# Softmax rows kept in SBUF, one undivided dq product, and seven zero stores at other places in the order of SP

## The chip, the cores and the metric

The kernel runs on one core of a Trainium2 chip. The core has five engines with an instruction stream each: TensorE (PE, with its weight loads as PEld), VectorE (DVE), ScalarE (ACT), GpSimd (POOL) and SyncE (SP). SP issues nearly all DMAs of this kernel, in program order; 16 DMA engines carry them out. SBUF is the memory on chip, with 128 partitions; PSUM takes the results of matmuls, and DVE or ACT copies ("evicts") them to SBUF. The metric is the time of one execution on the device in microseconds. Three runs of the kernel before took 430.75, 432.07 and 433.14 us; the median is 432.07. The profile is of one more execution.

## What is computed

Two layers of attention and two of a dense network, all with the same weights, for one token, forward and backward:

```
def _A_ref(x, k_cache, v_cache, wq, wo):        # Hq 32, Hkv 4, Dh 128, W 4096 of Sk 32768
    q = (x @ wq) as heads
    k, v = the last W rows of k_cache and v_cache, each for 8 heads
    p = softmax(q k^T * Dh ** -0.5)
    return (p v) @ wo
def _B_ref(x, w1, b1, w2):                      # D 1024, F 3584
    h = x @ w1 + b1
    return (h * tanh(softplus(h))) @ w2
x = x + _A_ref(layernorm(x), ...)   # A1
x = x + _B_ref(layernorm(x), ...)   # B2
x = x + _A_ref(layernorm(x), ...)   # A3
x = x + _B_ref(layernorm(x), ...)   # B4
outputs: x, and the gradients of x, k_cache, v_cache, wq, wo, w1, b1, w2 for a given grad_out
```

The gradients are large: dwq and dwo have 8.4 MB each, dw1 and dw2 7.3 MB each in bf16. Those of the caches have 33.6 MB each. Only their last 4096 rows of each head are computed (4.2 MB each); the other 58.7 MB are zeros that have to be written.

## The kernel before

**Stages.** The order of all instructions is written out by hand. It runs A1 forward (`attn_fwd`), B2 forward (`mlp_B2_fwd`), A3 forward, B4 forward and backward together (`mlp_B4`), A3 backward (`attn_bwd`), B2 backward (`mlp_B2_bwd`), A1 backward, and then the weight gradients as outer products. In the profile, B2 forward lies at about 70 to 111 us, A3 forward at 112 to 148, B4 at 148 to 219, A3 backward at 219 to 247, B2 backward at 247 to 295, A1 backward from 295 on. Products with one token are memory-bound: each weight matrix is read once for one column. In the stages from A3 on PE also transposes matrices in SBUF (`T8`, `fill`), which the backward products need.

**Zero stores.** The 112 pieces of zeros, 512 KB each, are `zero_jobs`. `zeros(n)` (L140) issues the next n of them on SP, from a place in SBUF that holds zeros (`zsrc`). They have no due time, so they are placed by hand wherever DMA has room: after loads, between blocks of B4 (`ZB4`), between steps of the attention (the `Z_` lists), between chunks of the w2 pass (the dictionary passed to `w2_pass`, L598), and between pieces of the w1 pass (L849).

**Loads.** Weights are loaded in an order that is fixed in `queue`. A load is issued as soon as its slot in a ring of buffers is free (`rel`, `pump`). SP issues in order, so a load stands behind all zero stores that were put before it, and at most eight DMAs of SP are under way, since each waits for the eighth before it.

**w2 pass and w1 pass.** `w2_pass` goes over w2 in 14 chunks of 512 KB: four matmuls, eight transposes with an ACT eviction, a multiply-and-sum on DVE (L596), then eight matmuls for the chunk before, after which its slot is released and `zeros(Z_.get(c, 0))` is called. The w1 pass of B2 backward goes over w1 in 16 pieces of 448 KB in the same way, with no R product.

**Softmax rows.** The backward pass of an attention layer needs its softmax matrix `p` (128 x 1024 bf16, 256 KB). The tile `misc` has three such places: `sB`, `sA` and `zlo`, the last of which holds zeros. A1 writes p to `sA`, which POOL copies to DRAM (`p1_d`, L551). A3 writes p to `sB`. In A3 backward p of A3 goes to DRAM too (`p3_d`, L787) and p of A1 comes back into `sB` (L788); in A1 backward p of A3 comes back into `wo[:, 0, :]` (L759), since the outer products for dV need both.

**Last stage.** In A1 backward `wo_dead` makes the list `jobs` of outer products. A job is four (`w2`, `w1`) or more matmuls with two contracted rows, into PSUM banks that `p_bank` hands out, and as many evictions of 128 x 512 to a staging buffer, shared between DVE (L896) and ACT (L899) by `ev_out`. When a buffer is full, SP stores it (L984 for dw2, L1002 for dw1, L1103 for the caches, L971 for dwo, L1007 for dwq). dw2 has 14 jobs, in seven pairs; a pair ends with two stores of 512 KB. Each pair carries one zero store behind it (the `z` of `add`, L1080, issued in `run_jobs`). `out_step` (L1110) runs jobs inside A1 backward: step 0 issues eight pieces of zeros as five stores, step 3 runs two jobs, step 4 one job after every eighth matmul of dq (L805 to L811), steps 5 and 6 two each. The rest runs after A1 backward.

**dq** is called here the product of dqpair with wq (L805): 64 matmuls, two for each head, that accumulate in the bank `R`. `d_cols` (L404) evicts R and folds it; the backward layer norm follows.

Of the kernel before, what the change touches and what calls it, by code (L numbers as in the profile page):

```python
# [21 lines left out]
def kernel(  # L22
# [42 lines left out]
    keep = ctx.enter_context(tc.tile_pool(name="keep", bufs=1))  # L65
    dram = ctx.enter_context(tc.tile_pool(name="dram", bufs=1, space=bass.MemoryType.DRAM))
    pt = ctx.enter_context(tc.tile_pool(name="pt", bufs=3, space=bass.MemoryType.PSUM))
# [18 lines left out]
    jk = kt([P, WC], BF16, "jk")  # L86
    misc = kt([P, 3072], BF16, "misc")
    sB, sA, zlo, zt = misc[:, 0:1024], misc[:, 1024:2048], misc[:, 2048:3072], misc[:, 1024:3072]
    Kf = K[:].rearrange("p g t d -> p g (t d)")
    Kl = K[:].rearrange("p g t d -> p (g t d)")  # L90
    Vf = V[:].rearrange("p g t d -> p g (t d)")
    kpf = kp[:].rearrange("p j x -> p (j x)")
    jkf = jk[:].bitcast(FP32)

# [5 lines left out]
    v_v = A_v_cache[0, :, Sk - W:, :].rearrange("g (p t) d -> p g t d", p=P)  # L100
    p1_d = dram.tile([P, WC], BF16, name="p1_d")
    p3_d = dram.tile([P, WC], BF16, name="p3_d")

# [19 lines left out]
    make_identity(nc, ident_bf[:])  # L123
    ident_f = kt([P, P], FP32, "ident_f")
    make_identity(nc, ident_f[:])
    nc.gpsimd.memset(zlo, 0.0)
# [176 lines left out]
    gmask = kt([P, G], FP32, "gmask")  # L303
    pat = kt([P, NC, 32], FP32, "pat")
    npair = kt([P, 4, TD], BF16, "npair")
# [16 lines left out]
    def constants():  # L322
        nc.vector.reduce_sum(fold[:], ident_f[:].rearrange("p (c x) -> p x c", c=NC), axis=AX.X)
        nc.vector.tensor_copy(pat[:], fold[:, None, :].to_broadcast([P, NC, 32]))
# [12 lines left out]

    wt = {}
    wk_n = dict(h=TF, hm=TF, u=TF, w_=TF, r=TF, t_f=TF, dact=8)
    cols1 = kt([P, 32], FP32, "cols1")  # L340
# [121 lines left out]
    def attn_fwd(x_col, l, first, p_dst, F_, Z_):  # L462
# [41 lines left out]
        mps = sm_tile(1, P)  # L504
        mm(mps[:], nm[:], ident_f[:], True, True)
        m32 = kpf.bitcast(FP32)[0:1, 0:P]
        nc.vector.tensor_reduce(out=m32[:].rearrange("p (c x) -> p c x", c=NC),
# [11 lines left out]
        tps = sm_tile(P, 1)  # L519
        mm(tps[:], pat[:].rearrange("p c x -> p (c x)"), sw[:], True, True)  # L520
        rT = wk("rT", 1)
# [28 lines left out]
        if first:  # L550
            nc.gpsimd.dma_start(p1_d[:], sA)  # L551
            rel("r2", 0)
# [13 lines left out]

    def mish(h, a_bf, dact, n):
        hm, u, w_, r = wk("hm", n), wk("u", n), wk("w_", n), wk("r", n)
        t_f, v1, v2 = wk("t_f", n), hm, w_
        nc.vector.tensor_scalar(out=hm[:], in0=h, scalar1=20.0, scalar2=None, op0=ALU.min)  # L570
        nc.scalar.activation(u[:], hm[:], ACT.Exp)
        nc.vector.scalar_tensor_tensor(out=w_[:], in0=u[:], scalar=2.0, in1=u[:], op0=ALU.add, op1=ALU.mult)
        nc.vector.tensor_scalar(out=r[:], in0=w_[:], scalar1=2.0, scalar2=None, op0=ALU.add)
        nc.vector.reciprocal(r[:], r[:])
        nc.vector.tensor_mul(t_f[:], w_[:], r[:])
        ga = nc.vector.tensor_mul(a_bf, h, t_f[:])
        nc.vector.scalar_tensor_tensor(out=v1[:], in0=t_f[:], scalar=1.0, in1=r[:], op0=ALU.add, op1=ALU.mult)
# [58 lines left out]
    def mlp_B2_fwd(x_col):  # L636
# [13 lines left out]
        zeros(2)  # L650
        h = wk("h", TF)
        nc.vector.tensor_add(h[:], hacc[:], b1_f[:])
        dact = kt([P, TF], FP32, "dact_B2")
        mish(h[:], apair[:, 1, :], dact[:], TF)
        sv["dact"] = dact
        R, dps, ds = w2_pass(apair[:, 1, :], gpair[:, LI["B4"], :], {8: 1, 9: 1, 10: 1, 11: 1})
        nc.gpsimd.memset(sA, 0.0)
        zsrc[:] = [zt, 2048]
        da4 = kt([P, TF], FP32, "da4")
# [6 lines left out]
    def mlp_B4(x_col, da4):  # L666
# [23 lines left out]
        def sel(b):  # L690
            full = b < 3
            nh, nk = (2, 8) if full else (1, 4)
            hps = sm_tile(P, 8)
            for cc in range(2):
                for tt in range(2):
                    k = 2 * cc + tt
                    mm(hps[:, k:k + 4 * (nh - 1) + 1:4], jkf[:, cc * 256 + tt:cc * 256 + tt + 255:2], selD[:] if full else sel1[:], k == 0, k == 3)
            h = wk("h", nk)
            nc.vector.tensor_add(h[:], hps[:, 0:nk], b1_f[:, 8 * b:8 * b + nk])
            hcol[b] = h  # L700

        def act(b):
            nk, f0 = 8 if b < 3 else 4, 8 * b
            dact = wk("dact", nk)
            mish(hcol[b][:], apair[:, 0, f0:f0 + nk], dact[:], nk)
            nc.vector.tensor_mul(hpair[:, 0, f0:f0 + nk], da4[:, f0:f0 + nk], dact[:])
            nc.vector.tensor_mul(dh[:, f0:f0 + nk], da4[:, f0:f0 + nk], dact[:])
            spent(2.8, 0.2)
# [34 lines left out]
        for i in range(2):  # L743
            mm(dn[:].rearrange("p (a i) -> p i a", i=2)[:, i, :], jkf[:, i * P:(i + 1) * P], ident_f[:, 0:P:32], i == 0, i == 1)
        tt = wk("xx", 2 * TD)
# [3 lines left out]
    def attn_bwd(g_col, g_bf, l, sv, last, nxt, F_, Z_, step):  # L749
# [6 lines left out]
        if last:  # L756
            p_t, ds_t = sB, wo[:, 1, :]
            wo_dead()
            nc.gpsimd.dma_start(wo[:, 0, :], p3_d[:])  # L759
        else:  # L760
            p_t, ds_t = sv["p"], sA
        zeros(Z_[0])
        acc = one_tile("acc", HQ)
        j_cols(big, acc, 8, F_[0], True)
        do32 = wk("do32", HQ)
        nc.vector.tensor_copy(pad[:, :, 0:8], acc[:].rearrange("p (g h) -> p g h", g=G))
# [18 lines left out]
        sv["p"], sv["ds"] = p_t, ds_t  # L785
        if not last:
            nc.gpsimd.dma_start(p3_d[:], sB)  # L787
            nc.gpsimd.dma_start(sB, p1_d[:])  # L788
            sv["p"] = wo[:, 0, :]
        step(1)  # L790
# [14 lines left out]
        for h in range(HQ):  # L805
            for hf in range(2):
                g = 2 * hf + h % 2
                mm(R[32 * g:32 * g + 32, :].rearrange("p (t d) -> p t d", t=4), bc(dqpair[:, LI[l], h:h + 1]),
                   wq[:, 4 * hf:4 * hf + 4, h * P:(h + 1) * P], h < 2, h >= HQ - 2, tile_position=(0, 32 * g))
            if h % 4 == 3 and h < 31:  # L810
                step(4)  # L811
        y = d_cols(R, hook=lambda: step(5))
# [4 lines left out]
    def mlp_B2_bwd(g_col, g_bf, sv, x3):  # L817
        bcast_g(g_bf)
        R, dps, ds = w2_pass(apair[:, 0, :], g_bf, {10: 1})
        zeros(3)  # L820
        dh = kt([P, TF], FP32, "dh_B2")
# [21 lines left out]
        def pairs(i, w, ring, sl):  # L843
# [4 lines left out]
            rel(ring, sl)  # L848
            zeros({9: 2, 12: 1, 14: 1}.get(i, 0))  # L849

# [9 lines left out]
        n3 = nv[:].rearrange("p (t h) -> p t h", h=2)  # L860
        t3 = wk("t3", TD)
        nc.vector.tensor_add(t3[:], n3[:, :, 0], n3[:, :, 1])
# [171 lines left out]
    def wo_dead():  # L1034
# [43 lines left out]
        for n in range(NW2 // 2):  # L1078
            add("w2a", n, lambda c=2 * n: pair_half(row_sp["w2"], c, w2_out, w2_lhs, 0))
            add("w2", n, lambda c=2 * n: pair_half(row_sp["w2"], c, w2_out, w2_lhs, 1), 1)  # L1080
        for n in range(16):
# [28 lines left out]
    def out_step(i):  # L1110
# [62 lines left out]
```

## Time and profile before

| | us |
|---|---|
| median of 3 runs | 432.07 |
| profiled execution | 431.02 |
| its span, first to last instruction | 429.2 |
| busy: PE, DVE, ACT | 321.2, 234.4, 219.1 |
| q1, SP's DMA queue, 168.84 MB: share of the 16 engines' span | 99.2% |
| one dw2, dwo or dk/dv store (512 KB), median to landing | 9.4 (all from wo), 7.1 (K) |
| chain: share of DMA, PE, ACT, DVE | 40%, 35%, 11%, 7% |
| last eviction ends | 413 |

A DMA's time to landing has its time in the queue in it. The DMA share in the windows is the time that packets took, as a share of 16 engines; it does not tell slow packets from full ones, so it is read together with the GB/s. The releaser of a wait is inferred from semaphores.

### The profile page before, as it was taken

The numbers are of one execution on the slowest core, as the hardware profiler recorded it, in microseconds if no ns is written. First come the engines' busy times: TensorE is split into PE (matmuls) and PEld (weight loads), VectorE is DVE, ScalarE is ACT, GpSimd is POOL, SyncE is SP. The second block draws the span as 40 slices with busy tenths as digits, with TensorE's granted clock in tenths as the row PEclk, the third lists the DMA queues.
The fourth block names the chain that finished last, engine by engine and source line by source line (L and its number), as shares of the span: only waits on it lengthen the run. The fifth ranks groups of instructions, "written<-read, shape, count | busy, mean of one in ns | idle before, by whom it ended". The sixth has DMA issues, their size and how long they took to land.

```text
span 429.2 us, 9216 instructions
## 1 busy us (share of the span) xinstructions
PE 321.2 (75%) x3732; PEld 188.3 (44%) x3732; DVE 234.4 (55%) x532; ACT 219.1 (51%) x335; POOL 15.4 (4%) x54
## 2 busy tenths in 40 slices
PE   3476736367697898878788898887799799999830
PEld 1154315345455587756646565764423223321100
DVE  2035102068535346555537288673367998899940
ACT  1036101036436356646534267482487699999940
POOL 2000000000000000000000000000400111000000
PEclk9999555569889979999989989685955555555555
DMA  8999999999999999999999999999999999999995
GB/s 329 423 419 419 411 408 399 406 407 378 387 418 409 417 417 365 417 409 384 381 408 406 350 397 386 373 362 421 411 421 417 419 413 413 403 409 412 410 413 242
DMA packets 49975, 170.50 MB, mean 397 GB/s; under 512 B 4848, under 2 KB 5900, under 8 KB 45836
## 3 DMA queue, kind: packets, MB, share of 16 engines
q1 hardware_dynamic: 49456, 168.84, 99.2%
q0 software_dynamic: 416, 1.06, 0.7%
q8 instruction: 29, 0.48, 0.4%
q14 instruction: 14, 0.11, 0.1%
q10 hardware_dynamic: 60, 0.01, 0.0%
HBM read 70.79 MB, written 99.10 MB: 396 GB/s over the span
## 4 chain that ended last, share of the span: by engine, by line
DMA 40%; PE 35%; ACT 11%; DVE 7%; issue 3%; SPq 0%; ACTq 0%; DVEq 0%
DMA K<-in_B_w_dram 9%; DMA wo<-in_A_wo_dram 8%; PE tp L264 8%; PE R L244 7%; DMA out_dram<-misc 7%; DMA K<-in_A_k_cache_dram 5%; DMA wo<-in_B_w_dram 4%; PE sm L244 4%; PE acc L244 4%; ACT wo L899 4%; PE op L244 3%; ACT K L237 3%; PE lo L244 3%; DMA out_dram<-wo 3%; ACT wq L899 3%
## 5 line engine op out<-in xcount | busy, mean ns | idle before, releaser
L237 ACT COPY K<-tp 128x1024 bf16<-128x1024 bf16 x60 | 58.8, 1016 | 14.3 <-PE tp L264 13.3
L264 PE MATMUL tp<-ident_bf,K 128*128 128x128 bf16 x656 | 52.0, 238 | 6.4 <-ACT K L237 2.8
L244 PE MATMUL op<-wo 2*128 2x512 bf16 (+2 forms) x123 | 52.1, 562 | 5.0 <-ACT wo L899 2.7
L244 PEld LDWEIGHTS <-wo 128*128 128x128 bf16 (+2 forms) x590 | 24.4, 101 | 61.8 <-issue 53.5
L264 PEld LDWEIGHTS <-K 128*128 128x128 bf16 x656 | 44.3, 109 | 12.7 <-issue 9.6
L237 ACT COPY wo<-tp 128x1024 bf16<-128x1024 bf16 x33 | 33.5, 1023 | 25.7 <-PE tp L264 22.9
L899 ACT CAST wo<-op 128x512 bf16<-128x512 f32 (+1 forms) x51 | 31.2, 629 | 7.9 <-DMA out_dram<-wo 1.8
L596 DVE CUSTOM_DVE_ANT_0 K<-K,kp 128x1024 bf16<-128x1024 bf16 (+1 forms) x22 | 24.6, 1127 | 2.8 <-PE R L244 1.0
L235 DVE COPY jk<-R 128x512 f32<-128x512 f32 (+1 forms) x11 | 7.3, 665 | 33.9 <-PE R L244 33.9
L264 PE MATMUL tp<-ident_bf,wo 128*128 128x128 bf16 x336 | 24.4, 226 | 0.6 <-ACT wo L237 0.5
L244 PE MATMUL acc<-wo 2*128 2x512 bf16 (+1 forms) x41 | 24.3, 593 | 0.2 <-DVE V L896 0.2
L244 PE MATMUL hi<-wo 2*128 2x512 bf16 x41 | 24.3, 592 | 0.0
L244 PE MATMUL lo<-wo 2*128 2x512 bf16 x41 | 24.1, 587 | 0.0
L264 PEld LDWEIGHTS <-wo 128*128 128x128 bf16 x336 | 20.1, 101 | 6.9 <-issue 6.8
L237 ACT CAST jk<-hi 128x512 bf16<-128x512 f32 x4 | 2.6, 661 | 37.7 <-PE hi L244 37.7
L244 PE MATMUL sm<-wo 2*128 2x512 bf16 (+1 forms) x33 | 19.8, 600 | 1.3 <-DVE cols L384 1.3
L896 DVE CAST wo<-op 128x512 bf16<-128x512 f32 (+1 forms) x32 | 18.4, 599 | 4.1 <-PE tp L930 1.5
L235 DVE CAST jk<-lo 128x512 bf16<-128x512 f32 x4 | 2.8, 711 | 31.9 <-PE lo L244 31.9
L235 DVE COPY K<-tp 128x1024 bf16<-128x1024 bf16 x22 | 14.9, 690 | 9.6 <-PE tp L264 9.5
L244 PE MATMUL R<-wo 2*128 2x512 bf16 (+1 forms) x33 | 19.6, 593 | 0.6 <-DVE wo L896 0.4
L237 ACT COPY wq<-tp 128x1024 bf16<-128x1024 bf16 x13 | 13.0, 1018 | 11.7 <-PE tp L264 8.8
L364 ACT ACTIVATE cols<-cols,eps_t 128x1 f32<-128x1 f32 x4 | 1.2, 294 | 33.4 <-DVE cols L361 33.4
(293 smaller groups left out, 656.2 us busy)
## 6 DMA issues: line engine op xcount, KB each, us to landing
out_dram<-misc SPq DMA_DIRECT2D x97, 512.0 KB, 10.2
out_dram<-wo SPq DMA_DIRECT2D x39, 512.0 KB, 9.4
K<-in_B_w_dram SPq DMA_DIRECT2D x28, 512.0 KB, 8.1
K<-in_A_k_cache_dram SPq DMA_DIRECT2D x9, 1024.0 KB, 14.9
wq<-in_A_wq_dram SPq DMA_DIRECT2D x8, 1024.0 KB, 10.0
out_dram<-wq SPq DMA_DIRECT2D x8, 1024.0 KB, 13.5
K<-in_B_w_dram SPq DMA_DIRECT2D x16, 448.0 KB, 6.1
out_dram<-wo SPq DMA_DIRECT2D x16, 448.0 KB, 7.2
```

Source lines behind the costliest of these rows:

```text
L235: return nc.vector.tensor_copy(out_ap, in_ap)
L237: return nc.scalar.copy(out_ap, in_ap)
L244: return nc.tensor.matmul(out_ap, lhsT=lhsT, rhs=rhs, start=start, stop=stop, skip_group_check=True, **kw)
L264: nc.tensor.transpose(ps[:, b * P:(b + 1) * P], ap, ident_bf[:])
L364: nc.scalar.activation(lnv[:], var[:], ACT.Ln, bias=eps_t[:, 0:1], scale=1.0)
L596: return nc.vector.tensor_tensor_reduce(out=w, in0=w, in1=vec, scale=1.0, scalar=0.0, op0=ALU.mult, op1=ALU.add, accum_out=acc_col)
L896: nc.vector.tensor_copy(out_ap, in_ap)
L899: nc.scalar.copy(out_ap, in_ap)
```

## The change

The rows: `misc` gets a fourth place, `sC`, for p of A1; p of A3 stays in `sB`. The tiles in DRAM and the four copies by POOL are gone. To make room, the float identity lies in a part of `kp` and is made again after the B2 forward w2 pass (`make_identity`, on POOL), a 128 x 4 selector `sel4` stands in for its strided use, `pat` is replaced by four products with `fold`, and the temporaries of `mish` and `do32` lie in `kp` and `jk`.

The order: step 4 of `out_step` is no longer called, so the 64 matmuls of dq follow each other, behind the two jobs of step 3. The seven dw2 pairs carry no zero store. One more piece of zeros is issued at chunk 2 of the B2 forward w2 pass, two more in A3 backward after dqpair is set off (Z_[2], 3 to 5), one at chunk 1 of the B2 backward w2 pass, two more between w2 pass and w1 pass (3 to 5), and one at piece 4 of the w1 pass. `ZB4` goes from 12, 11, 9, 7 to 11, 11, 10, 7.

```diff
-    misc = kt([P, 3072], BF16, "misc")
-    sB, sA, zlo, zt = misc[:, 0:1024], misc[:, 1024:2048], misc[:, 2048:3072], misc[:, 1024:3072]
+    misc = kt([P, 4096], BF16, "misc")
+    sB, sA, zlo, zt, sC = misc[:, 0:1024], misc[:, 1024:2048], misc[:, 2048:3072], misc[:, 1024:3072], misc[:, 3072:4096]
-    p1_d = dram.tile([P, WC], BF16, name="p1_d")
-    p3_d = dram.tile([P, WC], BF16, name="p3_d")
-    ident_f = kt([P, P], FP32, "ident_f")
-    make_identity(nc, ident_f[:])
+    ident_f = kpf[:, 512:768].bitcast(FP32)
+    make_identity(nc, ident_f)
+    sel4 = kt([P, 4], FP32, "sel4")
...
-        mm(tps[:], pat[:].rearrange("p c x -> p (c x)"), sw[:], True, True)
+        for c in range(NC):
+            mm(tps[32 * c:32 * c + 32, :], fold[:], sw[:], True, True, tile_position=(0, 32 * c))
...
         if first:
-            nc.gpsimd.dma_start(p1_d[:], sA)
             rel("r2", 0)
...
-    def mish(h, a_bf, dact, n):
-        hm, u, w_, r = wk("hm", n), wk("u", n), wk("w_", n), wk("r", n)
-        t_f, v1, v2 = wk("t_f", n), hm, w_
+    def mish(h, a_bf, dact, n, tmp):
+        hm, u, w_, r, t_f = [tmp[:, i * n:(i + 1) * n] for i in range(1, 6)]
+        v1, v2 = hm, w_
...
-        R, dps, ds = w2_pass(apair[:, 1, :], gpair[:, LI["B4"], :], {8: 1, 9: 1, 10: 1, 11: 1})
+        R, dps, ds = w2_pass(apair[:, 1, :], gpair[:, LI["B4"], :], {2: 1, 8: 1, 9: 1, 10: 1, 11: 1})
         nc.gpsimd.memset(sA, 0.0)
+        make_identity(nc, ident_f)
...
-            p_t, ds_t = sB, wo[:, 1, :]
+            p_t, ds_t = sC, wo[:, 1, :]
             wo_dead()
-            nc.gpsimd.dma_start(wo[:, 0, :], p3_d[:])
...
-        do32 = wk("do32", HQ)
+        do32 = jkf[:, P:P + HQ]
...
-        if not last:
-            nc.gpsimd.dma_start(p3_d[:], sB)
-            nc.gpsimd.dma_start(sB, p1_d[:])
-            sv["p"] = wo[:, 0, :]
...
-            if h % 4 == 3 and h < 31:
-                step(4)
...
-        R, dps, ds = w2_pass(apair[:, 0, :], g_bf, {10: 1})
-        zeros(3)
+        R, dps, ds = w2_pass(apair[:, 0, :], g_bf, {1: 1, 10: 1})
+        zeros(5)
...
-            zeros({9: 2, 12: 1, 14: 1}.get(i, 0))
+            zeros({4: 1, 9: 2, 12: 1, 14: 1}.get(i, 0))
...
-            add("w2", n, lambda c=2 * n: pair_half(row_sp["w2"], c, w2_out, w2_lhs, 1), 1)
+            add("w2", n, lambda c=2 * n: pair_half(row_sp["w2"], c, w2_out, w2_lhs, 1))
...
-            run_jobs(1 if i == 4 else 2)
-
-    ZB4 = [12, 11, 9, 7]
+            run_jobs(2)
+
+    ZB4 = [11, 11, 10, 7]
...
-    x1, sA1 = attn_fwd(x0, "A1", True, sA, [0] * 6, [0] * 4)
+    x1, sA1 = attn_fwd(x0, "A1", True, sC, [0] * 6, [0] * 4)
...
-    g2, g2b, _ = attn_bwd(g3, g3b, "A3", sA3, False, "B2", [4, 3, 5, 2], [3, 1, 3], lambda i: None)
+    g2, g2b, _ = attn_bwd(g3, g3b, "A3", sA3, False, "B2", [4, 3, 5, 2], [3, 1, 5], lambda i: None)
```

More of the change, by code (lines that the diff above doesn't have):

```diff
@@ L65 @@
     keep = ctx.enter_context(tc.tile_pool(name="keep", bufs=1))
-    dram = ctx.enter_context(tc.tile_pool(name="dram", bufs=1, space=bass.MemoryType.DRAM))
     pt = ctx.enter_context(tc.tile_pool(name="pt", bufs=3, space=bass.MemoryType.PSUM))
@@ L92 @@
     kpf = kp[:].rearrange("p j x -> p (j x)")
-    jkf = jk[:].bitcast(FP32)
+    jkf, kpf32 = jk[:].bitcast(FP32), kpf.bitcast(FP32)
     wq_v = A_wq.rearrange("(t p) j -> p t j", p=P)
@@ L303 @@
     gmask = kt([P, G], FP32, "gmask")
-    pat = kt([P, NC, 32], FP32, "pat")
     npair = kt([P, 4, TD], BF16, "npair")
@@ L322, in constants @@
     def constants():
-        nc.vector.reduce_sum(fold[:], ident_f[:].rearrange("p (c x) -> p x c", c=NC), axis=AX.X)
-        nc.vector.tensor_copy(pat[:], fold[:, None, :].to_broadcast([P, NC, 32]))
+        nc.vector.reduce_sum(fold[:], ident_f.rearrange("p (c x) -> p x c", c=NC), axis=AX.X)
+        nc.vector.tensor_copy(sel4[:], ident_f[:, 0:P:32])
         nc.vector.reduce_sum(gmask[:], fold[:].rearrange("p (g h) -> p g h", g=G), axis=AX.X)
@@ L338 @@
     wt = {}
-    wk_n = dict(h=TF, hm=TF, u=TF, w_=TF, r=TF, t_f=TF, dact=8)
+    wk_n = {}
     cols1 = kt([P, 32], FP32, "cols1")
@@ L504, in attn_fwd @@
         mps = sm_tile(1, P)
-        mm(mps[:], nm[:], ident_f[:], True, True)
-        m32 = kpf.bitcast(FP32)[0:1, 0:P]
+        mm(mps[:], nm[:], ident_f, True, True)
+        m32 = kpf32[0:1, 0:P]
         nc.vector.tensor_reduce(out=m32[:].rearrange("p (c x) -> p c x", c=NC),
@@ L650, in mlp_B2_fwd @@
         zeros(2)
-        h = wk("h", TF)
-        nc.vector.tensor_add(h[:], hacc[:], b1_f[:])
+        h = jkf[:, 0:TF]
+        nc.vector.tensor_add(h, hacc[:], b1_f[:])
         dact = kt([P, TF], FP32, "dact_B2")
-        mish(h[:], apair[:, 1, :], dact[:], TF)
+        mish(h, apair[:, 1, :], dact[:], TF, jkf)
         sv["dact"] = dact
-        R, dps, ds = w2_pass(apair[:, 1, :], gpair[:, LI["B4"], :], {8: 1, 9: 1, 10: 1, 11: 1})
+        R, dps, ds = w2_pass(apair[:, 1, :], gpair[:, LI["B4"], :], {2: 1, 8: 1, 9: 1, 10: 1, 11: 1})
         nc.gpsimd.memset(sA, 0.0)
+        make_identity(nc, ident_f)
         zsrc[:] = [zt, 2048]
@@ L697, in sel @@
                     mm(hps[:, k:k + 4 * (nh - 1) + 1:4], jkf[:, cc * 256 + tt:cc * 256 + tt + 255:2], selD[:] if full else sel1[:], k == 0, k == 3)
-            h = wk("h", nk)
-            nc.vector.tensor_add(h[:], hps[:, 0:nk], b1_f[:, 8 * b:8 * b + nk])
+            h = kpf32[:, 64 * (b % 2):64 * (b % 2) + nk]
+            nc.vector.tensor_add(h, hps[:, 0:nk], b1_f[:, 8 * b:8 * b + nk])
             hcol[b] = h
@@ L703, in act @@
             nk, f0 = 8 if b < 3 else 4, 8 * b
[L704 to L707, printed above, removed]
+            tmp = kpf32[:, 64 * (b % 2):64 * (b % 2) + 64]
+            dact = tmp[:, 6 * nk:7 * nk]
+            mish(hcol[b], apair[:, 0, f0:f0 + nk], dact, nk, tmp)
+            nc.vector.tensor_mul(hpair[:, 0, f0:f0 + nk], da4[:, f0:f0 + nk], dact)
+            nc.vector.tensor_mul(dh[:, f0:f0 + nk], da4[:, f0:f0 + nk], dact)
             spent(2.8, 0.2)
@@ L743, in mlp_B4 @@
         for i in range(2):
-            mm(dn[:].rearrange("p (a i) -> p i a", i=2)[:, i, :], jkf[:, i * P:(i + 1) * P], ident_f[:, 0:P:32], i == 0, i == 1)
+            mm(dn[:].rearrange("p (a i) -> p i a", i=2)[:, i, :], jkf[:, i * P:(i + 1) * P], sel4[:], i == 0, i == 1)
         tt = wk("xx", 2 * TD)
@@ L860, in mlp_B2_bwd @@
         n3 = nv[:].rearrange("p (t h) -> p t h", h=2)
-        t3 = wk("t3", TD)
+        t3 = wk("t2", TD)
         nc.vector.tensor_add(t3[:], n3[:, :, 0], n3[:, :, 1])
```

## The prediction

> **What bounds the kernel now.** I read the page first: DMA by slices, the queues, the chain by engine.
>
> ```profile
> GB/s 329 423 419 419 411 408 399 406 407 378 387 418 409 417 417 365 417 409 384 381 408 406 350 397 386 373 362 421 411 421 417 419 413 413 403 409 412 410 413 242
> q1 hardware_dynamic: 49456, 168.84, 99.2%
> q0 software_dynamic: 416, 1.06, 0.7%
> HBM read 70.79 MB, written 99.10 MB: 396 GB/s over the span
> DMA 40%; PE 35%; ACT 11%; DVE 7%; issue 3%; SPq 0%; ACTq 0%; DVEq 0%
> ```
>
> The 16 DMA engines are occupied from the first load to the last store, and most slices move 405 to 423 GB/s: bytes set the time. But six slices lie at 350 to 381, so there is room for stores in some places, and only 40% of the chain is DMA, so other work paces stretches of it. q0 is the queue of the four softmax-row copies. Next, the windows by stage (columns: length, busy us of PE, PEld, DVE, ACT, POOL, then TensorE clock, DMA share, GB/s):
>
> ```profile
> 90.00:115.00 25.00, 18.88 (x290) 13.40 (x290) 20.46 (x47) 14.17 (x14) 0.95 (x1) 0.91 1.01 386
> 235.00:250.00 15.00, 11.92 (x167) 7.52 (x164) 5.75 (x14) 3.39 (x5) 0.55 (x1) 0.93 0.98 365
> 250.00:268.00 18.00, 15.79 (x262) 10.99 (x263) 16.38 (x29) 14.17 (x14) 0.00 (x0) 0.96 1.01 390
> 268.00:292.00 24.00, 19.95 (x268) 17.38 (x268) 16.94 (x37) 15.74 (x17) 0.00 (x0) 0.72 1.01 373
> 303.00:338.00 35.00, 30.54 (x258) 11.33 (x247) 22.67 (x48) 23.22 (x42) 3.10 (x18) 0.64 1.03 418
> 338.00:380.00 42.00, 38.81 (x232) 11.81 (x229) 38.48 (x77) 36.62 (x74) 4.27 (x17) 0.50 1.02 411
> 380.00:413.00 33.00, 28.94 (x115) 5.92 (x112) 31.61 (x52) 33.00 (x68) 0.00 (x0) 0.50 1.02 413
> 413.00:424.50 11.50, 0.00 (x0) 0.00 (x0) 0.00 (x0) 0.06 (x1) 0.00 (x0) 0.50 0.99 405
> ```
>
> The first four rows are the stages that read w2 and w1 for B2, and the dq stage of A3: their rates are 365 to 390. From 303 on the rate is full, and after the engines stop at 413 DMA needs another 11.5 us. But DVE and ACT are nearly full too from 338. Two limits lie close together there. Last, the timeline around dq and the stores:
>
> ```profile
> 240.18 3.64 PE L244 MATMUL R<-wq,dqpair 128*32 128x512 bf16 x64
> 313.79 1.04 PE L244 MATMUL R<-wq,dqpair 128*32 128x512 bf16 x8
> 314.77 0.60 PE L244 MATMUL op<-wo 2*128 2x512 bf16 x1
> 329.42 0.69 DVE L896 CAST wo<-op 128x512 bf16<-128x512 f32 x1 [1.18 <-DMA out_dram<-wo]
> 331.82 1.57 SPq L984 DMA_DIRECT2D out_dram<-wo  x2
> 333.44 1.19 SPq L151 DMA_DIRECT2D out_dram<-wo  x1
> 356.51 4.85 SPq L1103 DMA_DIRECT2D out_dram<-V  x4
> 361.48 4.88 SPq L1002 DMA_DIRECT2D out_dram<-wo  x4
> ```
>
> dq of A3 took 3.64 us in one piece at full clock; dq of A1 runs as eight groups of 8, some 0.97 us apart from the next work, at half clock. Each pair of dW2 chunks is stored with one zero store behind it. Four stores occupy SP for 4.85 us, 1.2 each: SP is held to the pace of the DMA engines (512 KB in 1.25 us). And a DVE eviction waited 1.18 us for a staging buffer that a store still held.
>
> **The change, part by part.** All times on the profiled execution (span 429.2, 431.02 in all, 1.05 under the median 432.07).
>
> *Softmax rows.* Four copies of 256 KB go (L551, L787, L788, L759): 1.05 MB, at 413 GB/s 2.5 us of DMA. Three, 1.9 us, lie before 303; the fourth, 0.6, is at 303. The first lies in 5 to 90 us, which runs at 413 GB/s, so 0.6 us comes straight off. The rest counts as DMA time in the sum.
>
> *Seven zero stores* leave the last stage: 7 x 1.25 = 8.75 us of DMA there. With the row copy the last stage loses 9.35 us of DMA.
>
> *The same seven earlier.* By the order of SP: one between the w2 loads of the B2 forward (about 98 us); the twelve after B4's first block become eleven and the nine after its third ten, so that one store moves some 30 us later and past the loads of block 1 and 2; two more behind the first seven w2 loads of the B2 backward (246 us); one after its chunk 1; two more before the w1 pass (269); one after its piece 4. Loads are queued behind them on SP, and the chain waits for these loads: it has 6.93 us on one of them from 256.4 and 6.94 on one from 282.9. So each store costs 1.25 us unless DMA had room. Room against 415 GB/s: 25 x 29/415 = 1.75 us in the first window, 1.8, 1.1 and 2.4 in the next three, 7.0 in all. How much of that can be filled the trace does not say: slow packets or idle engines look alike in it (share 0.98 to 1.01). Bounds 0 and 7.0. I take 4.35: the one store at 98 fits wholly in its 1.75; half of 2.9 for the three of the w2 pass, whose loads from chunk 7 on already come 1.28 us apart; 1.6 of 2.4 in the w1 pass, where the evictions and not the loads set the pace until 280. So at 303 the chain is late by 8.75 - 1.9 - 4.35 = 2.5 us (bounds 6.85 and -0.15).
>
> *dq in one piece.* Before, the last pair of dW2 is issued at 336.98. After: two jobs on PE (310.9 to 312.4), then 64 matmuls. Between 3.64 us (row of A3) and 8 x 0.97 = 7.8 (half clock). I take 5.4: the clock has just fallen there, and the dense run that starts at 295.77 goes from 0.43 us for each four to 0.22 at 299.14, 3.4 us later; 3.4 us at 0.121 are 28 matmuls, the other 36 take 2.0. The upper bound has a row for it: from 310 to 338 PE was busy 25 of 28 us and the clock stood at 0.55. [...] Dq ends at 317.8, its eight evictions done under it. Then 12 jobs, 48 evictions: DVE starts one each 0.60, ACT each 0.49, so 0.27 together at best; 42 us for 120 in the next stage are 0.35 with all else. At 0.31 they take 14.9; one more for the eviction of R: 333.7. The engines are 3.3 us earlier (bounds -0.5 and 5), and waits for staging buffers such as the 1.18 go with it; I take 3.5. What dq had covered: PE's K=2 products; they are now behind it, and who would wait is DMA. The eight stores of zeros issued at 303.6 hold it until about 320; the next pair of data comes at 321 or so, so up to 1.5 us of DMA may stand idle there.
>
> *What the last stage can give.* From 338 to 380 stores land 7.1 us after issue, some 5.7 in flight at 1.25 each. A cushion of three is needed (at 200 to 205 us, with three left, the rate fell to 321), so 7.1 - 3 x 1.25 = 3.4 us of lag can go before DMA waits for the engines. Dwo and dwq are 16.8 MB, 41 us of DMA, and the engines make them in 33: that phase stays DMA's, and its end moves with its start. So the end moves by 3.5 + 3.4 = 6.9, under the 9.35 that bytes alone would give (bounds 3.4 and 9.35). [...]
>
> *Small edits.* Four 32-column products replace the one with pat (0.25 us of PE each piece, twice in the kernel): +0.3 us each on the softmax sum, beside zero stores in A3 and row loads of wo in A1; without that cover 0.6. Mish's temporaries in kp and jk, sel4 for the strided identity: same counts and shapes, 0. The new identity on POOL (0.5 us) has some 20 us before its reader. The eviction of R now waits for POOL's copy of do too, which in the last stage ends at 304 against 309: 0.
>
> Sum: -6.9 + 2.5 = -4.4 us: 426.6 on the profiled execution, **427.7** against the median.
>
> **Rivals.**
> *Even exchange.* The low rates are slow packets, not room: late by 6.85 at 303, and 6.9 back at the end: 0, 432.0. For it: DMA share near 1.0 in all four windows, and w2 loads already 1.28 us apart. Against: the rate of 331 to 360 from 235 to 245, where SP issued nothing for 6 us.
> *Slower.* The last stage is the engines' own: dq in one piece leaves DVE and ACT idle for 5 us and nothing comes of the staging waits, so the start of dwo does not move, and only the 3.4 us of lag go, while the stores cost their 6.85 earlier: +3.4, 435.5. It decides if dW2's last pair is issued no earlier after dq's start than before (26 us) and less than 3.4 us of room is filled. For it: ACT 33.00 of 33 us. Against: both evicting engines idle 12 of 35 us from 303 to 338, and DVE waits for stores there.
> *Bytes alone.* All 7.0 filled and DMA never waits: -9.4, 422.7. For it: full rate throughout 303 to 413. Against: the cushion.
> *It doesn't do what it says:* the rows could still be held up by a wait for the zero stores that read the same tile. The waits are unchanged but for those of POOL's queue, so I give it 0.02, time as before.
>
> **How the numbers follow.** A measurement of this kernel tells 0.5%, 2.2 us, from no change. Forecast 0.56 (its own range 425 to 430), even exchange 0.17, slower 0.15, bytes alone 0.10, not done 0.02. Faster is 0.56 + 0.10 = 0.66; same 0.19; slower 0.15. The range of 422.5 to 433 holds the first, second and fourth and cuts the outer part of the slower one.
>
> **What would show it.** Queue q0 shrinks from 1.06 MB to the small outputs. In the windows, the B2 backward (w2 and w1) ends 2 to 3 us later relative to its start and moves more GB/s; if it is over 5 us later, the room was not there. Dq is one row of 64 matmuls of 4 to 6 us. The last dW2 store is issued 20 to 24 us after dq's first matmul. After 338 SP's stores wait for evictions and land in under 7.1 us; a tail after the last eviction of 8 to 9 us in place of 11.5. The forecast is wrong if the tail is as long as before, or the start of dwo is no earlier.

## The result, and the profile after

| | before | after |
|---|---|---|
| median, 20 runs each (us) | 432.52 (430.75 to 434.19) | 435.01 (432.45 to 437.97) |
| profiled execution / its span | 431.02 / 429.2 | 436.97 / 435.2 |
| first store of step 0 in A1 backward | 303.6 | 313.9 |
| from there to the last eviction | 109.5 | 107.0 |
| from the last eviction to the end of the span | 16.1 | 14.3 |

The changed kernel is slower: ratio 1.005, 95% interval 1.0033 to 1.0068. The forecast of 427.7 was wrong.

The profiled execution of the changed kernel lies 1.96 us above its median, that of before 1.5 below. So the two traces differ by 6.0 us and the medians by 2.5. Sizes are therefore taken below from experiments whose profiled executions lie within half a microsecond of their medians, where there are such.

The page of the changed kernel: DMA by slices, the queue of the row copies, and the chain by engine (which this time accounts for about half of the span only, so its shares can't be set beside those of before):

```profile
GB/s 318 425 420 416 409 407 397 409 399 364 358 418 404 417 416 384 392 356 388 373 416 404 363 396 391 334 400 419 411 424 358 368 301 404 385 374 410 411 412 323
...
q0 software_dynamic: 96, 0.01, 0.0%
HBM read 70.27 MB, written 98.58 MB: 388 GB/s over the span
...
PE 20%; DMA 13%; ACT 10%; DVE 4%; issue 2%; SPq 1%; ACTq 0%; DVEq 0%
```

The row copies are gone (q0 moved 1.06 MB before). But the rate over the span fell from 396 to 388, the early slices are no fuller, and there are new dips at 358, 368 and 301 from 326 us on, where before every slice but the last moved over 400.

Windows of the changed kernel (columns as before: length, busy us of PE, PEld, DVE, ACT, POOL, clock, DMA share, GB/s). The first four rows are the same stretches as before; the next four are those of before set 10.3 us later, as A1 backward now starts that much later:

```profile
90.00:115.00 25.00, 20.10 (x273) 14.27 (x274) 19.81 (x41) 14.31 (x15) 1.27 (x3) 0.71 0.99 364
235.00:250.00 15.00, 11.87 (x179) 8.03 (x175) 6.48 (x14) 4.74 (x6) 0.00 (x0) 1.00 1.00 375
250.00:268.00 18.00, 13.03 (x184) 8.85 (x184) 12.02 (x22) 9.70 (x10) 0.00 (x0) 0.82 1.03 402
268.00:292.00 24.00, 17.85 (x248) 14.54 (x244) 15.60 (x33) 13.04 (x15) 0.00 (x0) 0.78 0.99 363
313.30:348.30 35.00, 28.93 (x262) 11.58 (x254) 23.86 (x51) 24.20 (x46) 2.51 (x17) 0.73 0.95 385
348.30:390.30 42.00, 39.62 (x232) 12.28 (x231) 38.55 (x77) 37.43 (x77) 4.48 (x17) 0.50 0.93 365
390.30:423.30 33.00, 26.46 (x106) 5.38 (x103) 29.45 (x49) 30.60 (x63) 0.00 (x0) 0.50 1.02 411
423.30:433.00 9.70, 0.00 (x0) 0.00 (x0) 0.00 (x0) 0.00 (x0) 0.00 (x0) 0.50 0.98 401
```

Two things are to be seen. In the w2 pass (250 to 268) the engines got through less: PE 184 matmuls where there were 262, ACT 10 instructions where there were 14. The stores went in, and the loads and the work behind them came later. (Of the delay 2.8 us lie ahead of this stage: its first w2 load is issued at 240.73, before at 237.90.) And in the last stage the DMA engines now wait: 385 and 365 GB/s where it was 418 and 411. The DMA share says the same: it fell from 1.03 and 1.02 to 0.95 and 0.93, which is 35 x 0.08 + 42 x 0.09 = 6.6 us of DMA time that nothing uses, out of the 9.35 us of transfers that were taken away there.

How the stores hold the loads up, in the timeline of SP in the changed kernel (start, length, instructions):

```profile
242.20 3.65 SPq L180 DMA_DIRECT2D K<-in_B_w_dram  x5
246.17 5.58 SPq L147 DMA_DIRECT2D out_dram<-misc  x5
254.38 1.62 SPq L180 DMA_DIRECT2D K<-in_B_w_dram  x2
256.05 0.89 SPq L147 DMA_DIRECT2D out_dram<-misc  x1
257.10 15.97 SPq L180 DMA_DIRECT2D K<-in_B_w_dram  x9
```

The five stores at 246.17 (three before the change) and the one at 256.05 (new) stand ahead of the loads of the next chunks. On DVE, in the same kernel, the multiply-and-sum of the w2 pass shows what follows (the bracket is the idle time before):

```profile
259.48 1.23 DVE L593 CUSTOM_DVE_ANT_0 K<-K,kp 128x1024 bf16<-128x1024 bf16 x1
...
264.19 1.22 DVE L593 CUSTOM_DVE_ANT_0 K<-K,kp 128x1024 bf16<-128x1024 bf16 x1 [3.47 <-PE R L242]
```

DVE stands still for 3.47 us. It waits for PE, and PE for a load, as PE's waits from 245 to 280 say (us in all, times, longest):

```profile
PE R L242 <- DMA K<-in_B_w_dram: 4.5, 3, 3.5
```

The same view of a kernel with the rows kept on chip and the stores where they were (e1_rows_only below):

```profile
PE R L242 <- DMA K<-in_B_w_dram: 0.5, 1, 0.5
```

### The profile page after: what moved, and what is told of

It reads as the page before. It is cut to its first block, busy times and chain, and to the rows that moved or that the text cites. A ratio compares the mean times of both kernels' runs of the same rounds, so it can differ in the third digit from the quotient of the medians.

```text
span 435.2 us, 9224 instructions
## 1 busy us (share of the span) xinstructions
PE 321.5 (74%) x3744; PEld 190.7 (44%) x3744; DVE 233.3 (54%) x532; ACT 218.5 (50%) x335; POOL 13.6 (3%) x52
## 4 chain that ended last, share of the span: by engine, by line
PE 20%; DMA 13%; ACT 10%; DVE 4%; issue 2%; SPq 1%; ACTq 0%; DVEq 0%
DMA out_dram<-misc 7%; ACT wo L891 5%; DMA K<-in_B_w_dram 5%; PE R L242 5%; PE op L242 3%; PE tp L262 3%; ACT wq L891 3%; PE acc L242 3%; DMA K<-in_A_k_cache_dram 2%; PE sm L242 2%; PE lo L242 1%; ACT K L235 1%; PE hi L242 1%; PE tp L922 1%; DVE wo L888 1%
## 5 line engine op out<-in xcount | busy, mean ns | idle before, releaser
L262 PE MATMUL tp<-ident_bf,K 128*128 128x128 bf16 x656 | 53.6, 241 | 9.6 <-DMA K<-in_B_w_dram 4.2
L242 PE MATMUL op<-wo 2*128 2x512 bf16 (+2 forms) x112 | 47.3, 542 | 5.9 <-ACT wo L891 2.5
L242 PEld LDWEIGHTS <-wo 128*128 128x128 bf16 (+2 forms) x558 | 23.0, 102 | 51.3 <-issue 42.9
L262 PE MATMUL tp<-ident_bf,wo 128*128 128x128 bf16 x336 | 26.6, 238 | 0.6 <-ACT wo L235 0.5
L262 PEld LDWEIGHTS <-wo 128*128 128x128 bf16 x336 | 22.1, 107 | 7.6 <-issue 7.3
L242 PE MATMUL hi<-wo 2*128 2x512 bf16 x40 | 23.0, 574 | 0.0
L233 DVE COPY wo<-tp 128x1024 bf16<-128x1024 bf16 x19 | 12.8, 689 | 11.8 <-PE tp L262 11.7
L235 ACT COPY wq<-tp 128x1024 bf16<-128x1024 bf16 x13 | 13.0, 1019 | 11.8 <-PE tp L262 9.0
L242 PE MATMUL R<-wo,operm 128*32 128x512 bf16 x128 | 13.3, 564 | 7.1 <-DMA wo<-in_A_wo_dram 6.8
L242 PE MATMUL acc<-wo 2*128 2x512 bf16 (+1 forms) x32 | 18.3, 572 | 0.0
L242 PEld LDWEIGHTS <-npair 128*32 128x32 bf16 x184 | 5.8, 108 | 26.2 <-issue 21.8
```

What stands on the lines that cost most here:

```text
L233: return nc.vector.tensor_copy(out_ap, in_ap)
L235: return nc.scalar.copy(out_ap, in_ap)
L242: return nc.tensor.matmul(out_ap, lhsT=lhsT, rhs=rhs, start=start, stop=stop, skip_group_check=True, **kw)
L262: nc.tensor.transpose(ps[:, b * P:(b + 1) * P], ap, ident_bf[:])
```

## The experiments

They take the change apart into its three pieces (rows, dq, stores) and then vary the number of stores that are moved. Ratios are to the kernel before, run beside them on the same chip (medians 432.76 for the first four, 432.62 for the others; e1 to e4, e5 to e8 and e9 to e11 ran on three different chips, so between these groups the ratios are the fairer comparison). All points in time in the table are us of the profiled execution: the first store of A1 backward ("late stage starts"), from there to the last eviction, and from there to the end of the span. The column "B2 backward" is the time from the issue of its first w2 load to the start of the late stage. Six of the seven stores are issued inside it, and it leaves out what B4 does.

| kernel | median | ratio (95%) | B2 backward | late stage starts | to last eviction | to the end |
|---|---|---|---|---|---|---|
| before | 432.52 | | 65.7 | 303.6 | 109.5 | 125.6 |
| after | 435.01 | 1.005 (1.0033 to 1.0068) | 73.1 | 313.9 | 107.0 | 121.3 |
| e1: rows alone | 429.75 | 0.9935 (0.9915 to 0.9955) | 65.1 | 302.3 | 109.2 | 125.4 |
| e2: rows and dq | 430.4 | 0.9943 (0.9921 to 0.9965) | 65.1 | 303.2 | 109.5 | 125.5 |
| e3: rows and stores | 435.6 | 1.0074 (1.005 to 1.0098) | 72.6 | 310.3 | 108.7 | 123.1 |
| e4: stores alone | 437.69 | 1.012 (1.0099 to 1.014) | 75.0 | 313.5 | 109.0 | 123.5 |
| e5: rows, three stores, two behind w2 loads | 431.39 | 0.9959 (0.994 to 0.9978) | 68.7 | 308.4 | 108.2 | 122.5 |
| e6: rows, three stores in the w1 pass | 429.9 | 0.9933 (0.9911 to 0.9955) | 71.0 | 307.8 | 107.6 | 121.9 |
| e7: rows, one store in B2 forward | 430.34 | 0.9952 (0.993 to 0.9974) | 65.3 | 303.5 | 108.4 | 124.7 |
| e8: rows, six stores the other way | 436.81 | 1.0086 (1.0053 to 1.0119) | 66.8 | 303.4 | 115.7 | 131.7 |
| e9: after, without the stores of step 0 | 435.29 | 1.0052 (1.003 to 1.0073) | | (about 311) | | |
| e10: after, without the seven stores | 425.28 | 0.9848 (0.9785 to 0.9912) | 65.9 | 302.1 | 107.0 | 121.2 |
| e11: e6 with dq in one piece | 430.64 | 0.9947 (0.9925 to 0.9969) | 68.7 | 304.7 | 107.8 | 122.8 |

e9's start is that of its dq (320.2) less the 8.8 us that lie between the two in the others.

### The three pieces

**e1_rows_only.** The changed kernel with dq in turns again and the seven stores back at the dw2 pairs:

```diff
+            if h % 4 == 3 and h < 31:
+                step(4)
-            add("w2", n, lambda c=2 * n: pair_half(row_sp["w2"], c, w2_out, w2_lhs, 1))
+            add("w2", n, lambda c=2 * n: pair_half(row_sp["w2"], c, w2_out, w2_lhs, 1), 1)
-            run_jobs(2)
+            run_jobs(1 if i == 4 else 2)
-    ZB4 = [11, 11, 10, 7]
+    ZB4 = [12, 11, 9, 7]
...
-        zeros(5)
+        zeros(3)
...
```

Expected:

> The changed kernel with dq interleaved with the dw2 jobs again and all seven zero stores back behind the dw2 pairs, ZB4 12, 11, 9, 7: only the softmax rows stay on chip. Theory A (the stores put earlier cost their DMA time and more there, the row copies were worth their 2.5 us): 2 to 3 us faster than before, ratio 0.993 to 0.995. Theory B (dq in one piece is the loss, by starving DMA in the last stage): the same here, since neither is left. If the row copies were hidden: ratio 1.000.

429.75: 3.0 us faster than before. The rows do what the bytes said, and the new small instructions cost nothing that shows.

**e2_rows_dq.** The stores back at the pairs, dq left in one piece (e1 without the first and third hunk shown). Expected:

> The changed kernel with only the seven zero stores back behind the dw2 pairs (ZB4 as before); dq stays in one piece. Theory A: within 1 us of the kernel with the rows alone, so ratio 0.993 to 0.998. Theory B: slower than the rows alone by 3 us or more, ratio above 1.000.

430.4, no different from e1 within the intervals. With the stores in the pairs, dq in one piece changes nothing: the late stage takes 125.5 us against 125.4.

**e3_rows_zeros.** The changed kernel with dq in turns again (of e1 only the first and third hunk shown). Expected:

> The changed kernel with only dq interleaved again (one dw2 job after every eighth matmul); the seven zero stores stay early. Theory A: still slower than before, ratio 1.003 to 1.008. Theory B: faster than before by 2 us or more, ratio under 0.996.

435.6: from e1 to e3 the seven stores cost 5.85 us in the medians and 5.7 in the traces. The late stage starts 8.0 later, and 2.3 come back in it. Their own DMA time is 8.75. The B2 backward, which holds six of them (7.5 us of DMA), takes 7.5 us more. Its first load and the first store of the late stage, in e1 and then in e3:

```profile
237.21 4.46 SPq L180 DMA_DIRECT2D K<-in_B_w_dram  x7
302.30 3.62 SPq L149 DMA_DIRECT2D out_dram<-wo  x5
...
237.71 6.09 SPq L180 DMA_DIRECT2D K<-in_B_w_dram  x7
310.30 2.64 SPq L149 DMA_DIRECT2D out_dram<-wo  x4
```

**e4_zeros_only.** The kernel before with only the seven stores moved:

```diff
-            add("w2", n, lambda c=2 * n: pair_half(row_sp["w2"], c, w2_out, w2_lhs, 1), 1)
+            add("w2", n, lambda c=2 * n: pair_half(row_sp["w2"], c, w2_out, w2_lhs, 1))
-    ZB4 = [12, 11, 9, 7]
+    ZB4 = [11, 11, 10, 7]
...
-        zeros(3)
+        zeros(5)
...
```

> The kernel before with only the seven zero stores and ZB4 placed as in the changed kernel; rows through DRAM, dq interleaved. Theory A: slower by 3 to 7 us (late by 7 to 10 us at the start of A1 backward, of which 3 to 5 come back at the end), ratio 1.007 to 1.016. Theory B: ratio 0.998 to 1.002, since what leaves the last stage pays for what enters earlier.

437.69, the slowest of all, 4.9 above before. The late stage starts 9.9 us later and gives back 2.1. So the stores alone make the loss, with or without the rows and with or without dq in one piece.

### How many stores, and where

**e5_three_w2, e6_three_w1, e7_one_fwd.** From e1, three, three and one of the seven moves, each with as many pairs that lose their store:

e5:

```diff
-        R, dps, ds = w2_pass(apair[:, 0, :], g_bf, {10: 1})
+        R, dps, ds = w2_pass(apair[:, 0, :], g_bf, {1: 1, 10: 1})
-    g2, g2b, _ = attn_bwd(g3, g3b, "A3", sA3, False, "B2", [4, 3, 5, 2], [3, 1, 3], lambda i: None)
+    g2, g2b, _ = attn_bwd(g3, g3b, "A3", sA3, False, "B2", [4, 3, 5, 2], [3, 1, 5], lambda i: None)
```

e6:

```diff
-        zeros(3)
+        zeros(5)
-            zeros({9: 2, 12: 1, 14: 1}.get(i, 0))
+            zeros({4: 1, 9: 2, 12: 1, 14: 1}.get(i, 0))
```

e7:

```diff
-        R, dps, ds = w2_pass(apair[:, 1, :], gpair[:, LI["B4"], :], {8: 1, 9: 1, 10: 1, 11: 1})
+        R, dps, ds = w2_pass(apair[:, 1, :], gpair[:, LI["B4"], :], {2: 1, 8: 1, 9: 1, 10: 1, 11: 1})
-    ZB4 = [12, 11, 9, 7]
+    ZB4 = [11, 11, 10, 7]
```

> The kernel with the rows alone, with three of the seven zero stores moved early: two behind the first seven w2 loads of the B2 backward and one after its chunk 1; the last four dw2 pairs keep theirs. Theory A (no room in any of the three places: each store costs its 1.25 us where it is put and gives a third of that back at the end): 2 to 3 us slower than the rows alone, ratio to before 0.998 to 1.001, late by 3.5 to 4 us at the start of A1 backward. Rival (the room is missing in this place only): slower by the whole 5 to 6 us of the seven, ratio above 1.003.

> The rows alone, with three other stores moved early: two between the w2 pass and the w1 pass of the B2 backward, one after piece 4 of the w1 pass. Theory A: as the run before, ratio 0.998 to 1.001. Rival: there was room here (evictions paced the stage until 280 us), late by under 2 us at the start of A1 backward, ratio 0.992 to 0.995.

> The rows alone, with the one store at chunk 2 of the B2 forward w2 pass moved early and ZB4 11, 11, 10, 7. Theory A: about 1 us slower than the rows alone, ratio 0.995 to 0.997. Rival (it fits into the 1.75 us of room that the prediction saw): ratio 0.992 to 0.994.

Neither place in the B2 backward is cheap. The three stores of e5 make it 3.6 us longer than in e1, their own time being 3.75; the three of e6 make it 5.9 longer, and 3.6 in e11 below, which is the same program up to there. So executions of one program differ by some 2 us in this stretch. The profiled executions of e6 and e5 lie 1.6 and 1.3 us above their medians. What the one store in B2 forward costs does not show: the first w2 load of the B2 backward comes 1.0 later in e7 than in e1, but in the kernels without that store it lies anywhere from 236.0 to 239.7 (237.9 in the kernel before). The late stage gives back 0.7 us in e7, 3.5 in e6 and 2.9 in e5. That makes e6 equal to e1, and e5 1.6 slower in the medians. So e5 is faster than its theory A had it, and e6 has the ratio of its rival for another reason: there was no room early, but the late stage gave the time back. Three stores less give back as much as seven do (2.3 in e3), within some 1 us: the late stage has a limit of its own there.

**e8_six_later.** The opposite dose, from e1: six stores that before issued in A3 backward (three) and between w2 and w1 pass (three) go to the dw2 pairs, so that six of the seven pairs carry two:

```diff
-        zeros(3)
+        zeros(0)
-            add("w2", n, lambda c=2 * n: pair_half(row_sp["w2"], c, w2_out, w2_lhs, 1), 1)
+            add("w2", n, lambda c=2 * n: pair_half(row_sp["w2"], c, w2_out, w2_lhs, 1), 1 + int(n > 0))
-    g2, g2b, _ = attn_bwd(g3, g3b, "A3", sA3, False, "B2", [4, 3, 5, 2], [3, 1, 3], lambda i: None)
+    g2, g2b, _ = attn_bwd(g3, g3b, "A3", sA3, False, "B2", [4, 3, 5, 2], [3, 1, 0], lambda i: None)
```

> The rows alone, with the opposite dose: the three stores of A3 backward behind the w2 loads and the three between w2 pass and w1 pass go to the dw2 pairs too (two behind each but the first). If the last stage is DMA's and the early stages are too, nothing changes: ratio 0.992 to 0.996. If the early stages lose more to a store than the last stage gains without it (as with the seven): 4 to 6 us faster than the rows alone, ratio 0.980 to 0.985. If there was room early that is now lost: slower than the rows alone by 2 us or more, ratio above 0.998.

Of the three outcomes named it is the last: slower than the rows alone, by 7.1 us in the medians. The late stage starts no earlier (303.4; e1 302.3), though 7.5 us of transfers are gone ahead of it. The late stage takes 6.3 us more. The windows of e1 from 235 to 292, then those of this kernel, and two of its late stage:

```profile
235.00:250.00 15.00, 12.34 (x162) 7.64 (x163) 5.47 (x14) 3.46 (x6) 0.00 (x0) 0.90 1.03 378
250.00:268.00 18.00, 15.49 (x268) 10.92 (x264) 16.22 (x29) 13.70 (x14) 0.00 (x0) 0.99 1.01 381
268.00:292.00 24.00, 19.02 (x276) 16.05 (x276) 17.01 (x38) 16.86 (x18) 0.00 (x0) 0.77 1.03 399
...
235.00:250.00 15.00, 12.59 (x168) 8.00 (x161) 5.73 (x14) 3.81 (x5) 0.00 (x0) 0.85 0.87 336
250.00:268.00 18.00, 15.82 (x261) 11.10 (x258) 15.76 (x30) 13.15 (x14) 0.00 (x0) 0.93 0.84 309
268.00:292.00 24.00, 18.55 (x274) 15.79 (x275) 16.82 (x38) 16.81 (x18) 0.00 (x0) 0.82 0.87 325
303.00:338.00 35.00, 28.88 (x245) 10.90 (x238) 21.41 (x46) 22.53 (x41) 2.37 (x16) 0.66 1.02 420
338.00:380.00 42.00, 39.32 (x236) 11.55 (x234) 38.43 (x77) 35.76 (x72) 4.49 (x17) 0.50 1.02 413
```

This is what room looks like: the DMA share is 0.84 to 0.87, where it was 1.01 to 1.03 in e1, and the work of the engines is nearly the same (261 matmuls from 250 to 268; 268 in e1). The idle share makes 15 x 0.13 + 18 x 0.16 + 24 x 0.13 = 8.0 us, about the 7.5 that were taken out. So in e1 those stores had just about filled the room, and e3 and e5 show that nothing more went in. The kernel before has the same stores there, and a share of 0.98 to 1.01 at 365 to 390 GB/s.

### What sets the late stage

**e9_no_z8.** The changed kernel without the eight pieces of zeros (4.2 MB, 10 us of DMA) that step 0 of A1 backward issues. They are left out altogether, so that part of the output is not written:

```diff
+    del zero_jobs[-8:]
...
-            zeros(8)
```

> The changed kernel without the eight pieces of zeros that A1 backward issues at its step 0: they are left out and stay unwritten, 4.2 MB or 10 us of DMA less in the last stage. Theory A (with the seven stores gone the last stage is bound by its evictions, up to the tail): from dq's first matmul to the last eviction 97 to 99 us as in the changed kernel, the tail 14 us as there, so no more than 2 us faster than the changed kernel, ratio to before 1.000 to 1.005. Rival (the last stage still runs at the pace of DMA): 7 to 10 us faster than the changed kernel, ratio 0.982 to 0.990.

435.29: no gain. From dq's first matmul to the last eviction it takes 98.1 us, and 98.2 in the changed kernel. Two windows of this trace, the first from some 8 us ahead of its late stage:

```profile
303.00:338.00 35.00, 28.60 (x307) 12.94 (x308) 17.92 (x40) 18.97 (x32) 4.60 (x19) 0.79 0.65 259
338.00:380.00 42.00, 38.86 (x234) 11.58 (x232) 38.74 (x82) 37.66 (x76) 4.49 (x17) 0.50 0.95 372
```

DMA idles a third of the time from 303 to 338, and the end stays where it is. So the changed kernel's late stage is no longer set by DMA up to the last eviction. The engines set it, with DVE busy 38.74, ACT 37.66 and PE 38.86 of 42 us. In the changed kernel the chain from 345 to 421 holds no DMA either; it goes through evictions on ACT and DVE and matmuls on PE in turn. Whether the evictions bind or the matmuls, which run at a granted clock of 0.50 there, no run separates.

**e10_no_seven.** The changed kernel with the seven stores left out altogether (3.7 MB of output not written), and the rest placed as before, but for the counts of B4 (`ZB4` as changed):

```diff
+    del zero_jobs[-7:]
...
-        zeros(5)
+        zeros(3)
...
```

> The changed kernel without the seven stores anywhere: they are left out and stay unwritten. Theory A (they cost 8 to 10 us where the change puts them, as there was no room): A1 backward starts at 301 to 304 us as with the rows alone, the rest takes 121 to 123 us as in the changed kernel, 423 to 427 in all, ratio 0.980 to 0.988. Rival (something else in the changed kernel makes the early stages late, such as the new places of temporaries): start at 308 us or later, ratio above 0.993.

425.28, on four runs with a wide interval. The late stage starts at 302.1 as in e1 and takes 121.2 us as in the changed kernel. The seven stores cost about 10 us at their new places (9.7 in the medians; 11.8 between the traces, of which 2.2 are what these lie apart from their medians), and leaving their old ones is worth about 4 (125.5 in e2, with dq in one piece too, to 121.2). Even with room for all of them, the move could not have given 6.9 in the late stage.

**e11_dq_three_w1.** e6 with dq in one piece (the first and third hunk of e1 undone):

> A try for the best version: rows on chip, dq in one piece, three stores of the seven at the w1 pass as in the run of three there, four behind the last dw2 pairs. If dq in one piece gains where the last stage has fewer stores: ratio 0.988 to 0.992. If it is neutral: 0.992 to 0.995.

430.64, not to be told from e6 (429.9). Here, too, dq in one piece is worth nothing that shows, and the late stage takes 2.7 us less than with all seven stores in the pairs (122.8 against 125.5 in e2).

The fastest kernel that does all of the work is e1, the rows alone, and it beats the kernel before and the changed one: 0.9935 of before. e6 is equal to it and no better.

## Why the prediction was wrong

**Softmax rows: right.** 2.5 us of DMA were taken; e1 is 3.0 us faster (1.9 to 3.7 by the interval).

**Room for the seven stores: the step that failed.** The prediction took 4.35 us of the stores as filled into room, from bounds of 0 and 7.0. The stores alone were to make the late stage start 8.75 - 4.35 = 4.4 us later (2.5 with the 1.9 of the row copies). From e1 to e3, the pair of traces nearest to their medians, they made it come 8.0 us later: almost no room, at the lower bound. For the six in the B2 backward the prediction had some 3 us of room; with 7.5 us of DMA they made it 7.5 longer from e1 to e3 and 8.0 from e2 to the changed kernel. Between before and e4 it was 9.9, between e2 and the changed kernel 10.7; these traces lie 2.6 and 1.9 further apart than their medians, so 7.3 and 8.8 if that difference lies ahead of the late stage. The room had been worked out from GB/s against 415, where the DMA share beside it, 0.98 to 1.01, already said that the engines were occupied; the prediction had that share as the argument for its rival, the even exchange. It noted that slow packets and idle engines can't be told apart; e8 does tell them apart, and the share was right. The bandwidth alone misled: 365 to 390 GB/s at a share of 0.98 to 1.01 had no room in it, and 309 to 336 GB/s at a share of 0.84 to 0.87 (e8) did.

**dq in one piece: the matmuls right, the evictions mis-sized.** The 64 matmuls in the changed kernel's timeline of PE:

```profile
322.68 5.32 PE L242 MATMUL R<-wq,dqpair 128*32 128x512 bf16 x64
```

5.32 us, where 5.4 was taken. The granted clock was 1.00 when dq began, fell to 0.50 at about 322.8 and was back at 1.00 from about 326.2, some 3.4 us later. So the estimate of 5.4, worked out from the run of matmuls at 295.77 in the kernel before (clock 0.50 to 299.14, then 1.00), was met, and the upper bound of 7.8, at half clock throughout, was not. The clock does not fall just there in every run, though. In e2 dq took the same 3.64 us as dq of A3 in the kernel before, which ran at a clock of 1.00:

```profile
312.00 3.64 PE L242 MATMUL R<-wq,dqpair 128*32 128x512 bf16 x64
```

So 5.4 was right where the fall came at dq's start, as the prediction took it (the changed kernel). Why the clock fell there and not in e2, no run shows. In e2 dq took 1.7 us less than in the changed kernel, and the late stage was no shorter than in e1. In the changed kernel the last dw2 store is issued 22.9 us after dq's first matmul, where it was 24.6 before (the prediction's 26 counts from the two jobs ahead of dq): 1.7 us earlier in place of the 3.5 that were taken. The 48 evictions behind dq took the 17.7 us from 327.94 to 345.6, 0.37 each; the prediction took 0.31, between the best possible 0.27 and the 0.35 of the next stage. The row of the next stage was the nearer one. In time the whole edit shows nothing: +0.65 us from e1 to e2, +0.74 from e6 to e11, -0.59 from e3 to the changed kernel, none of which stands out from the spread of the runs (and the kernels of the last two pairs were not run beside each other).

**What the late stage gives: mis-sized, 6.9 taken, 4.3 measured** (125.6 to 121.3 us, and 2.3 without dq in one piece). The two terms of it were 3.5 for the engines and 3.4 for the lag of the stores. The engines gave 2.5 (109.5 to 107.0 up to the last eviction). The tail behind the last eviction fell from 16.1 to 14.3, so the lag gave 1.8. The stores from 350 to 421 in the changed kernel show the same:

```profile
DMA to landing us min/median/max: 2.3/5.5/11.4
```

The median was 7.3 before (340 to 413). Ahead of the dwo and dwq phase alone it went from 7.2 (340 to 380) to 4.8 (345 to 388). So about 2 us of lag went and not 3.4. The cushion of three stores was too small: DMA waited for the engines while stores still took 4.8 us to land, where the prediction had let it come down to 3.75. Its rate fell to 385 and then 365, and came back to 411 only in the dwo and dwq phase. The dwo and dwq phase moves what it moved before, and the engines make it faster than DMA stores it, as the prediction had it (share 1.02 at 411 GB/s from 390.3 to 423.3, with the last eviction 14.3 us ahead of the end; 1.02 at 413 from 380 to 413 before). So its end moves with its start, but for the 1.8 us of lag: the first dwo store is issued at 389.5, 7.8 us later than before (381.7), where the late stage began 10.3 later.

**The sum.** Step by step, from before to e1, e3 and the changed kernel, the medians go -3.0, +5.85 and -0.6. That these add up to +2.25 is no test of the account, since each step starts where the last one ended; the medians of the result differ by +2.5. The forecast of -4.4 missed by 6.9: 2.6 of it is what the late stage fell short of 6.9 in the traces, and so 4.3 is left for the early part, about all of the 4.35 that had been taken as room. The rival that was given 0.15 has the measured figure, 435.5. Its condition on the room held (less than 3.4 us filled), and so did its price for the stores; its other condition did not, as the last dw2 pair does come earlier, by 1.7 us. Its 3.4 us for the late stage is near the 4.3 by luck: it gave all of it to the lag, where 2.5 came from the engines and 1.8 from the lag. The even exchange fell because the late stage gave 4.3 and not 6.9. "Bytes alone" fell twice: neither was there room early, nor did DMA stay the limit late.

**Signs that were named.** The B2 backward ended over 5 us later relative to its start (the last load of the K cache, queued behind the w1 pass, is issued 10.6 us later, the first w2 load 2.8), which had been named as the sign that the room was not there. The dq row, the time to the last dw2 store and the landing time after 338 lay inside what was named, and the tail was shorter by 1.8 us where 2.5 to 3.5 was named. So the late half of the forecast pointed the right way at some 60% of its size, and the early half was wrong.

## What stays open

Why the packets from 235 to 292 are slower than 415 GB/s while the DMA engines are occupied (365 to 390 at a share of 0.98 to 1.01 in the kernel before) was not tried. Whether a moved store costs a little more than its own DMA time is not clear: the B2 backward grew by 3.6, 3.6 and 5.9 us for 3.75, by 7.5 and 8.0 for 7.5, and by 9.3 from before to e4, and the spread between executions is as large as what is over. What the one store in B2 forward costs lies inside that spread too. The profiled executions before and after differ by 3.5 us more than the medians; 2.8 us of their difference lie ahead of the first w2 load of the B2 backward, which comes at 240.7 in the changed kernel and at 236.1 in e9, which issues the same instructions up to there.

## What to carry to other kernels

In this kernel a rate below 415 GB/s was room only where the DMA share was below 1 as well: 365 to 390 at 0.98 to 1.01 (before) was none, 309 to 336 at 0.84 to 0.87 (e8) was. The test was to take transfers out of that stretch: it got idler by 8.0 us for 7.5 taken out and no shorter (the late stage starts at 303.4 in e8, 302.3 in e1), so it had been filled, and the stores that were added came on top (8.0 us in e3). In the late stage, where DMA and the engines are matched, taking transfers out paid only until the engines bound (4.3 us of 9.35 taken out). Putting stores in cost nearly all of their time (8.0 of 8.75 ahead of it in e3, 6.3 of 7.5 in it in e8), so this kernel gained from transfers that went away, as the row copies did (3.0 us in e1). And when a change has several pieces, each should be priced at the margin: with dq in turns, three stores less gave the late stage as much as seven did (2.9 and 3.5 against 2.3).

## What the runs showed of the hardware

The DMA engines were occupied all the time at rates that lie 13% apart: share 1.00 and 0.99 at 375 and 363 GB/s (235 to 250 and 268 to 292 in the changed kernel), and 1.02 at 411 (390 to 423). And stores put ahead of loads on SP in the B2 backward, where the share is about 1 (0.98 to 1.01 before, 1.01 to 1.03 in e1), made it longer by about the DMA time of the stores: by 7.5 (e3) and 8.0 us (the changed kernel) for six (7.5 of DMA), by 3.6 for three in two traces (e5 and e11, 3.75 of DMA) and by 5.9 in a third (e6).
